# A filter in steps of four rows, copies of every third product input by ScalarE, and a new order, in a tuned convolution and FFN kernel

## The chip, the core and the metric

The kernel runs on one core of a Trainium2 chip. The metric is device time in microseconds (us). The kernel before takes 191.32 us (median of 3 runs, 191.17 to 191.43). The engines are named as in the profile: PE is TensorE (matmuls; PEld its weight loads), DVE is VectorE, ACT is ScalarE, POOL is GpSimd, and SP issues most of the transfers (DMA).

## The reference

For 2048 rows of 640 columns in bfloat16, cut to what matters:

```python
xn = layernorm(A_q)
k_shift = sum over t of 0..3 of A_k shifted down by t rows * A_shift_k[:, t]     # short filter, 4 taps
u = k_shift * A_v
y = causal convolution of u with A_ssm_k along the 2048 rows (by FFT in the reference), in bf16
s = xn * (y + u * A_ssm_D)
g = silu(gelu(xn @ B_w1 + B_b1) @ B_w2 + B_b2)                                    # 640 -> 1728 -> 640
return A_q + s * g
```

## The kernel before

Rows are spread so that partition p holds rows 16p to 16p+15; `n2` is the row within a partition. Two kinds of work run side by side: the FFN, in four chunks of four rows per partition, and the long convolution, done as a Fourier transform of two stages by matrices of sines. Every piece of work is a *step*, a name with a number, and the string `PLAN` lists all steps. `tc.manual_schedule()` keeps that order, so each engine executes its own steps in the order of the plan, and waits at the head of its queue for what the step needs. Nothing overtakes on an engine, and SP issues its transfers in the plan's order too; at most eight of them are under way at a time, since each waits for the landing of the eighth before it.

The steps that the prediction speaks of:

- Loads by SP: `X` (a chunk of A_q), `K` (four rows of A_k a partition, K0 with the rows above), `V` (two rows of A_v), `C` (A_ssm_k, five blocks), `B` (second FFN weight).
- FFN: `tt`/`te` transpose the normalized rows; `h` is the first matmul (L498; five matmuls of 512 columns into one bank, a short one at L494) and `he` its gelu; `g` is the second matmul (L531, fourteen of 320 columns), `ge` its silu, `gm` the multiply into xn.
- Short filter: `cv` with number 8i+s is step s of block i (two rows here) on DVE: products of `kh` with the taps (L626), sums (L622), and in s = 7 the product with v (L615). `uc` is the result, `tm` a temporary, each in a *slot* of `area` of two rows. The taps stand spread over all partitions in `w_exp`: a matmul with a column of the identity makes each half (`tap`, L675), two taps in the opening and two in the late steps `em`, which `ee` copies out.
- Kernel side: `kt` transposes A_ssm_k (L571), `kc` copies out to `kT`, `d` (`add_d`, L672) adds the ssm_D term, `kf` is the first transform stage (L582), `ke` copies out, `ks` stores to DRAM, `fl` loads it back in another layout, `ff` is the second stage, `fe` copies out to `K`, and `mk` loads a copy `ks` of it with neighbouring partitions swapped.
- u side: `uf`, `ue`, `us`, `ml` in the same way, then `mu` the second stage. Its result stays in a PSUM bank; `mp` and `mq` (DVE, L704) multiply it with `K` and `ks` into the two halves of `p`; `ma` and `mb` are the first inverse stage, `me` copies out, `ms` stores.
- End: `yl` loads back, `y` is the second inverse stage (L745, L746), `yt` the gate, `yo`/`ga` add A_q, `ys`/`gs` store.

`ff`, `mu`, `ma` and `mb` come in 40 *units* of 512 columns each. One such step is four matmuls of 32x32 (L445), and `TURNS` says for each unit by how many blocks the output is turned against the input, so that units of different turns occupy different parts of the array. PSUM has eight banks; `one(key)` hands the next free one to a step, and the bank returns when its last reader has dropped it. A slot of `area` is handed out likewise by `Slots.take`, and `SPANNED` names the tiles whose two slots of a pair must lie near each other. `evac` (L143 on ScalarE, L144 on DVE) is the helper that copies PSUM out, as the letter behind a step says.

Of the kernel before, what the change touches and what calls it, by code (L numbers as in the profile page):

```python
# [10 lines left out]
F32 = mybir.dt.float32  # L11
# [6 lines left out]
P = 128  # L18
# [18 lines left out]
cv1 he4 he8 C2 cv0 h6 cv9 he5 lb1 he6 h7 cv2 h12 ln6.d h11 cv8 ln5.d ln4.a h9 he10 ln7.a tt8 he12 B1 cv17 he11 he9 cv3  # L37
he7 cv10 cv18 B0 cv11 cv4 cv19 cv20 tt9 s B2 tt6 tt7 te9.a g3 cv21 te6.d cv22 tt5 C1 ge3 C0 ws2 ss te7.d sm g2 g7 cv12
C3 C4 ge2 kt3 V3 kt5 te5.d kt8 V1 d kc5.d kt10 ws0 kt14 K2 ge7 kc3.a te8.d kc10.d kt0 cv5 kf10 kc8.a kc14.a kf24 kt12
ke24.a kt4 kc12.d kf31 V7 kt6 kf11 kf9 ke10.a K3 kc4.d ke31.a kc0.d ke11.a kf44 kf43 V2 ke44.d kt2 kc2.d kc6.a kf17 X3  # L40
ke9.a kf32 ke32.d kf30 kt11 kf42 kt13 kf37 kt7 kc11.d ke30.a ks10 ke17.a kf38 kc13.d V6 ke42.a ke43.a kt9 ke37.d kf16
kf1 kc7.d kt1 gm3.d kf12 ke38.a ke16.a kc9.d kf36 kt15 kf21 ke1.a ke36.a kc1.d kf6 kf29 gm7.d kc15.d kf39 kf25 ke21.a
X2 cv33 V5 kf20 ke6.a kf41 cv32 V0 cv6 cv24 ks12 ke29.a ks14 cv23 cv13 ke25.a cv34 kf15 ke15.a ke41.a cv56 ke20.a ks5
g5 ke12.a kf7 kf13 ge5 cv57 kf14 kf27 kf8 ke39.a ke27.a kf26 kf40 ke8.a cv41 g0 kf28 ke40.a ks13 ke26.a ke14.a cv40
uf13 kf34 ks3 ke7.a kf19 ge0 cv35 ks8 ue13.a kf18 kf35 ke13.a ke18.a ks4 kf45 g4 ke19.a ks6 gm5.d uf17 cv36 ke45.a kf33
ke34.a ke28.a ks9 ke35.a gm0.d kf0 ke33.a cv7 kf23 cv14 V4 cv58 kf47 cv37 ge4 ke23.a ke0.a kf5 kf22 g6 uf4 ks2 ks11
ke5.a cv42 ke47.a ke22.a ks7 ge6 kf4 kf46 uf5 cv15 ls10 ke4.a cv59 uf15 kf3 ke46.a ks15 kf2 cv38 ke3.a ks1 ke2.a cv25
g1 ue4.a uf0 ks0 ue5.a gm6.d fl0 uf3 ue15.a ue17.a ue3.a uf12 cv43 ue12.a uf14 ue14.a uf16 cv39 ue16.a ue0.a cv26 uf1
# [888 lines left out]
```

## Time and profile before

| | |
|---|---|
| median of the runs | 191.32 us |
| profiled execution | 191.78 us, span 189.8 us |
| busy PE, DVE, ACT, POOL | 183.3, 171.1, 159.1, 59.5 us |
| chain that ended last | PE 75%, DMA 16%, ACT 3%, DVE 2% |
| moved by DMA | 57.67 MB, mean 304 GB/s |
| granted PE clock | full in all slices |

The page sums each engine's busy time, cuts the span into 40 slices, and follows the work that ended last back from release to release. Instructions on one engine overlap a little at their ends, so the time from one start to the next is shorter than the mean duration of one. A busy share is a mean over stages; the windows of the prediction give it stage by stage.

### The profile page before, as it was taken

What the parts mean: (1) busy time and instruction counts of PE and PEld (TensorE: products, weight loads), DVE (VectorE), ACT (ScalarE), POOL (GpSimd) and SP (SyncE); (2) the same over time, 40 slices, a digit from 0 to 9 for tenths busy, and PEclk for the clock granted to TensorE, in tenths of its full rate; (3) what the DMA queues carried; (4) which work ended last, traced back from release to release, by engine and by line L of the source; (5) the groups of instructions that cost most, each with busy time, mean ns of one, the idle gap of its engine ahead of it and who ended that gap; (6) DMA issues with size and microseconds to landing.
All of it is one profiled execution on the core that took longest, in us unless ns stands there. A gap on an engine that the chain in (4) does not pass through costs nothing.

```text
span 189.8 us, 4853 instructions
## 1 busy us (share of the span) xinstructions
PE 183.3 (97%) x1811; PEld 110.0 (58%) x1811; DVE 171.1 (90%) x341; ACT 159.1 (84%) x307; POOL 59.5 (31%) x99
## 2 busy tenths in 40 slices
PE   7999999899999999999999999999999999999992
PEld 2486467787765544466665434467563544677671
DVE  6979999999999999899989999999999950689993
ACT  3469999999999999999988999998789599894031
POOL 8539200013546111266043300046159440001050
PEclk9999999999999999999999999999999999999999
DMA  6999999987998999798599899998988859992165
GB/s 186 397 376 311 363 359 405 380 340 231 391 352 329 254 382 378 234 386 337 178 335 318 266 301 337 310 353 287 343 298 284 287 178 290 402 394 114 38 256 195
DMA packets 26399, 57.67 MB, mean 304 GB/s; under 512 B 3016, under 2 KB 14857, under 8 KB 26376
## 3 DMA queue, kind: packets, MB, share of 16 engines
q1 hardware_dynamic: 21872, 39.65, 61.0%
q0 software_dynamic: 4320, 17.70, 25.1%
q8 instruction: 14, 0.23, 0.5%
q14 instruction: 9, 0.07, 0.1%
q10 hardware_dynamic: 184, 0.01, 0.1%
HBM read 33.76 MB, written 18.35 MB: 275 GB/s over the span
## 4 chain that ended last, share of the span: by engine, by line
PE 75%; DMA 16%; ACT 3%; DVE 2%; issue 1%; SPq 1%; DVEq 0%; ACTq 0%
PE banks L531 28%; PE banks L498 21%; DMA w_sb<-in_B_w_dram 11%; PE banks L582 9%; PE banks L445 8%; DMA area<-in_A_ssm_k_dram 5%; PE banks L746 2%; PE banks L745 2%; PE banks L571 2%; ACT area L143 2%; PE banks L482 1%; ACT hT L510 1%; PE banks L494 1%; DVE xn L555 1%; DVE xn L547 0%
## 5 line engine op out<-in xcount | busy, mean ns | idle before, releaser
L143 ACT CAST area<-banks 128x512 bf16<-128x512 f32 (+3 forms) x162 | 78.8, 618 | 5.5 <-PE banks L445 5.5
L531 PE MATMUL banks<-w_sb,hT 128*128 128x320 bf16 (+1 forms) x462 | 66.0, 295 | 0.1
L531 PEld LDWEIGHTS <-hT 128*128 128x128 bf16 x462 | 43.3, 98 | 19.5 <-issue 3.8
L498 PE MATMUL banks<-xnT,w_sb 128*128 128x512 bf16 x230 | 53.5, 379 | 0.0
L704 DVE TENSOR_TENSOR area<-banks,area 128x512 bf16<-128x512 f32 x80 | 48.6, 682 | 0.8 <-PE banks L445 0.4
L498 PEld LDWEIGHTS <-w_sb 128*128 128x128 bf16 x230 | 21.7, 98 | 25.6 <-issue 2.7
L510 ACT ACTIVATE hT<-banks,b_f 128x512 bf16<-128x512 f32 x52 | 33.9, 706 | 1.8 <-PE banks L498 1.0
L539 ACT ACTIVATE sl<-banks 128x320 bf16<-128x320 f32 (+1 forms) x33 | 14.9, 464 | 12.7 <-PE banks L531 10.9
L626 DVE TENSOR_TENSOR area<-area 128x1280 bf16<-128x1280 bf16 x32 | 25.3, 814 | 0.1
L622 DVE TENSOR_TENSOR area<-area 128x1280 bf16<-128x1280 bf16 x24 | 19.3, 816 | 0.0
L730 POOL DMA_DIRECT2D scrC<-area x16 | 11.8, 737 | 23.2 <-DMA area<-area 18.7
L754 DVE TENSOR_TENSOR area<-banks,xn 128x426 bf16<-128x426 f32 (+1 forms) x18 | 10.0, 595 | 9.1 <-PE banks L746 9.1
L597 POOL DMA_DIRECT2D scrK<-area x16 | 8.8, 555 | 28.7 <-DVE area L144 19.1
L445 PE MATMUL banks<-area,mats 32*32 32x512 bf16 x640 | 17.2, 380 | 0.0
L582 PE MATMUL banks<-area,WA 128*128 128x212 bf16 (+1 forms) x64 | 16.5, 299 | 0.0
L547 POOL TENSOR_TENSOR xn<-xn,sl 128x320 bf16<-128x320 bf16 x14 | 11.2, 808 | 15.6 <-ACT sl L539 10.2
L582 PE MATMUL banks<-area,WB 128*128 128x426 bf16 (+1 forms) x64 | 15.8, 299 | 0.0
L608 POOL DMA_DIRECT2D scrU<-area x16 | 8.6, 543 | 20.9 <-ACT area L143 14.5
L445 PEld LDWEIGHTS <-mats 32*32 32x32 bf16 x640 | 6.4, 88 | 10.1 <-issue 8.2
L763 POOL DMA_DIRECT2D out_dram<-area x6 | 3.3, 551 | 26.5 <-DVE area L759 26.5
L144 DVE CAST area<-banks 128x426 bf16<-128x426 f32 (+3 forms) x18 | 10.9, 611 | 0.7 <-ACT area L143 0.5
L452 DVE BATCH_NORM_STATS2 st<-xn 128x6 f32<-128x320 bf16 x24 | 10.4, 477 | 0.0
(108 smaller groups left out, 209.4 us busy)
## 6 DMA issues: line engine op xcount, KB each, us to landing
scrK<-area POOLq DMA_DIRECT2D x16, 320.0 KB, 4.0
scrU<-area POOLq DMA_DIRECT2D x16, 320.0 KB, 5.1
area<-scrK SPq DMA_DIRECT2D x16, 320.0 KB, 6.6
area<-area SPq DMA_DIRECT2D x32, 160.0 KB, 4.4
area<-scrU SPq DMA_DIRECT2D x16, 320.0 KB, 4.4
scrC<-area POOLq DMA_DIRECT2D x16, 320.0 KB, 4.6
area<-scrC SPq DMA_DIRECT2D x16, 320.0 KB, 6.9
area<-in_A_k_dram SPq DMA_DIRECT2D x4, 640.0 KB, 9.4
```

What stands on the lines that cost most here:

```text
L143: return nc.scalar.copy(out=out_ap, in_=in_ap)
L445: nc.tensor.matmul(out=out[b, :], lhsT=mats[a, m, a], rhs=rhs[a, :], start=start, stop=stop)
L498: nc.tensor.matmul(out=ps, lhsT=w1_sb[:, t, ft * P:(ft + 1) * P], rhs=xnT[:, t, :], start=(t == 0), stop=(t == DT - 1))
L510: nc.scalar.activation(out=hT[:, ft, :], in_=one(("h", i)), func=ACT.Gelu_apprx_tanh, bias=b1_f[:, ft:ft + 1], scale=1.0)
L531: nc.tensor.matmul(out=ps[:, 0:ws.stop - ws.start], lhsT=hT[0:M, ft, q * P:(q + 1) * P], rhs=w2_sb[0:M, ft, hs.start + ws.start:hs.start + ...
L539: nc.scalar.activation(out=sl[:, ws], in_=one(key)[:, 0:ws.stop - ws.start], func=ACT.Silu)
L547: mul.tensor_tensor(out=xr[:, ws], in0=xr[:, ws], in1=live["sl", i][:, ws], op=ALU.mult)
L582: nc.tensor.matmul(out=ps[:, dst], lhsT=(WA, WB)[r][:, n2, :], rhs=rows[:, n2 % 2, src], start=True, stop=True)
L622: nc.vector.tensor_tensor(out=uc, in0=uc, in1=tmp, op=ALU.add)
L626: nc.vector.tensor_tensor(out=tmp if s else uc, in0=kh[:, r0:r0 + KC, :], in1=w_exp[:, j:j + 1, :].to_broadcast([P, KC, D]), op=ALU.mult)
L704: nc.vector.tensor_tensor(out=p_part(i, x), in0=full(one(("mu", i)), i), in1=span(name, i), op=ALU.mult)
L730: nc.gpsimd.dma_start(out=pair_view(scrC)[g2], in_=pair(("c", g2)))
```

## The change

1. `cv` works on blocks of four rows. `quad` takes two slots and makes one access pattern of them (two pieces of two rows); `v`, `uc` and `tm` become SPANNED. There are 32 steps of 2560 elements for 64 of 1280. Their DVE lines are now L641 (products with the taps), L637 (sums) and L630 (times v).
2. Every third unit of u (2, 5, ... 38) gets a step `mv`: ScalarE copies it from PSUM into the half of `p` that `mq` will fill, the bank is free after that one use, and `mp` and `mq` (now L717) read the copy.
3. All four taps are made in the opening, in two rounds over the same four banks, and ScalarE copies them out at full width. `em` and `ee` are gone. Warm-up matmuls go from 6 + 7 to 6 + 2 + 2.
4. Biases of ScalarE are numbers in the instruction; three constant tiles and their memsets are gone.
5. `blocks` knows a form `f`, one full matmul, for units whose turn is 0; the plan marks 61 steps with it.
6. `PLAN` and `TURNS` are written anew. K1 moves from ahead of the C loads to behind them, evacuations and normalizations change between ScalarE and DVE, and the FFN steps are dealt out among the stages in another way.

The diff, cut to its core:

```diff
-WARM = (6, 7)
+WARM = (6, 2, 2)
...
-TURNS = "302320120133202130013212102100231320131321131323"
+TURNS = "303222211332100321313102031211323202233020231231"
...
-ir he0 X1 he1 he2 em6 he3 em7 w h13 em5 K1 ls5 ws1 ls4 ls7 em4 K0 h8 ee6.d ee4.a ls6 h10 ee7.a ee5.a he13 cv16 lv1 lr1
+he2 w X1 ls5 h12 h13 h10 C1 ws1 he12 he4 ls6 h9 ls7 he0 he5 ls4 s he10 he9 K0 lv1 B0 lr1 cv1 lb1 ln7.d ln4.d ln6.d he13
...
-    KV = NJ // KC * 7
+    KV = NJ // KR * 7
...
-    SPANNED = ("kin", "K", "ks", "uin", "c")
+    SPANNED = ("kin", "K", "ks", "uin", "c", "v", "uc", "tm")
...
+    def copied(i):
+        return i % 3 == 2
+
     def one(key):
-        return banks[:, ones.take(key, 2 if key[0] == "mu" else 1), :]
+        return banks[:, ones.take(key, 2 if key[0] == "mu" and not copied(key[1]) else 1), :]
...
-                                 bias=sin_bias[:])
+                                 bias=-math.pi * (1.0 - SIN_EPS))
...
-    def blocks(out, m, rhs, turn, start=True, stop=True):
+    def blocks(out, m, rhs, turn, form, start=True, stop=True):
+        t = int(TURNS[turn])
+        if form == "f" and not t:
+            nc.tensor.matmul(out=out, lhsT=mats[:, m, :], rhs=rhs, start=start, stop=stop)
+            return
...
+    def quad(name, i, uses=1):
+        a0, a1 = (slots.take((name, 2 * i + x), uses) for x in range(2))
+        v = area[:, 2 * a0:2 * a0 + 2, :]
+        return bass.AP(v.tensor, v.offset, [list(v.ap[0]), [2 * D * (a1 - a0), 2], [D, 2], [1, D]])
...
     def kv_step(i):
         i, s = divmod(i, 8)
-        uc = pair(("uc", i), 6)
+        uc = quad("uc", i, 6)
         if s == 7:
-            nc.vector.tensor_tensor(out=uc, in0=uc, in1=pair(("v", i)), op=ALU.mult)
-            slots.drop(("v", i))
+            nc.vector.tensor_tensor(out=uc, in0=uc, in1=quad("v", i), op=ALU.mult)
+            drop_quad("v", i)
             return
...
-            r0 = 3 + i * KC - j
-            nc.vector.tensor_tensor(out=tmp if s else uc, in0=kh[:, r0:r0 + KC, :],
-                                    in1=w_exp[:, j:j + 1, :].to_broadcast([P, KC, D]), op=ALU.mult)
+            r0 = 3 + i * KR - j
+            nc.vector.tensor_tensor(out=tmp if s else uc, in0=kh[:, r0:r0 + KR, :].rearrange("p (a b) d -> p a b d", a=2),
+                                    in1=w_exp[:, j:j + 1, None, :].to_broadcast([P, 2, 2, D]), op=ALU.mult)
...
-    def late_tap(i):
-        tap(i // 2, i % 2, one(("em", i)))
...
+    def u_copy(i):
+        nc.scalar.copy(out=p_part(i, 1), in_=full(one(("mu", i)), i))
+        ones.drop(("mu", i))
+
     def product(i, x):
         name = ("K", "ks")[x]
-        nc.vector.tensor_tensor(out=p_part(i, x), in0=full(one(("mu", i)), i), in1=span(name, i), op=ALU.mult)
+        u = p_part(i, 1) if copied(i) else full(one(("mu", i)), i)
+        nc.vector.tensor_tensor(out=p_part(i, x), in0=u, in1=span(name, i), op=ALU.mult)
         drop_span(name, i)
-        ones.drop(("mu", i))
+        if not copied(i):
+            ones.drop(("mu", i))
...
+        taps(0, 2)
+        warm(WARM[2])
...
+        tap_out(0)
+        tap_out(1)
         norm_dve(0)
         norm_dve(1)
         turn(0)
         turn(1)
-        for j in range(2):
-            for h in range(2):
-                tap(j, h, banks[:, 2 * j + 2 + h, :])
+        taps(2, 4)
```

Three places of the new order, each by the instructions of one engine. First SP in the opening, before: `xn` is A_q, `in_A_k` the K loads, `in_A_ssm_k` the C loads, `w_sb` from `in_B_w` the second FFN weight, `in_A_v` the V loads.

```order
L273 DMA xn<-in_A_q_dram 128x2560
L280 DMA area<-in_A_k_dram 128x2560
L278 DMA area<-in_A_k_dram 112x1920
L279 DMA area<-in_A_k_dram 15x1920
L280 DMA area<-in_A_k_dram 128x2560
L303 DMA area<-in_A_ssm_k_dram 128x2048
L307 DMA w_sb<-in_B_w_dram 128x5x640 x2
L307 DMA w_sb<-in_B_w_dram 128x3x640
L309 DMA w_sb<-in_B_w_dram 64x640
L310 DMA w_sb<-in_B_b_dram 1x640
L303 DMA area<-in_A_ssm_k_dram 128x2048 x4
L283 DMA area<-in_A_v_dram 128x1280 x2
```

The same place now, to the first load of V and the one behind it:

```order
L305 DMA area<-in_A_ssm_k_dram 128x2048
L280 DMA area<-in_A_k_dram 112x1920
L281 DMA area<-in_A_k_dram 15x1920
L282 DMA area<-in_A_k_dram 128x2560
L309 DMA w_sb<-in_B_w_dram 128x5x640 x2
L309 DMA w_sb<-in_B_w_dram 128x3x640
L311 DMA w_sb<-in_B_w_dram 64x640
L312 DMA w_sb<-in_B_b_dram 1x640
L305 DMA area<-in_A_ssm_k_dram 128x2048 x4
L282 DMA area<-in_A_k_dram 128x2560
L275 DMA xn<-in_A_q_dram 128x2560
L282 DMA area<-in_A_k_dram 128x2560
```

One K load stood ahead of the four C loads and stands behind them now: K3, a chunk of A_q and K1 follow, and after them a V load and K2. Second DVE around `add_d`, before; L622 and L626 are filter steps, `mats` the small matrices, the copies to `area` are `kc`.

```order
L626 TENSOR_TENSOR area<-area 128x1280
L144 COPY xnT<-banks 128x512
L622 TENSOR_TENSOR area<-area 128x1280
L144 COPY xnT<-banks 128x512
L425 TENSOR_TENSOR mats<-area 128x384
L622 TENSOR_TENSOR area<-area 128x1280
L144 COPY xnT<-banks 128x512
L672 TENSOR_TENSOR area<-area,dD_sb 128x5
L144 COPY area<-banks 128x640
```

The same place now:

```order
L641 TENSOR_TENSOR area<-area 128x2560
L146 COPY xnT<-banks 128x512 x3
L553 TENSOR_TENSOR xn<-xn,sl_463 128x320
L146 COPY area<-banks 128x640 x3
L553 TENSOR_TENSOR xn<-xn,sl_467 128x320
L146 COPY area<-banks 128x640 x3
L687 TENSOR_TENSOR area<-area,dD_sb 128x5
L553 TENSOR_TENSOR xn<-xn,sl_506 128x320
```

A filter step stood ahead of `add_d` (L672) with a copy between; now six copies of the transposed kernel and two multiplies stand between the last filter step and `add_d` (L687). Third DVE where the products begin, before:

```order
L704 TENSOR_TENSOR area<-banks,area 128x512
L475 TENSOR_SCALAR xn<-xn,mv_1156,rs_1435 128x640
L704 TENSOR_TENSOR area<-banks,area 128x512 x12
L475 TENSOR_SCALAR xn<-xn,mv_1156,rs_1435 128x640
L704 TENSOR_TENSOR area<-banks,area 128x512 x66
```

And now, some way into the same stage:

```order
L717 TENSOR_TENSOR area<-banks,area 128x512 x3
L481 TENSOR_SCALAR xn<-xn,mv_1178,rs_1421 128x640
L717 TENSOR_TENSOR area<-area 128x512
L717 TENSOR_TENSOR area<-banks,area 128x512
L481 TENSOR_SCALAR xn<-xn,mv_1178,rs_1421 128x640
L717 TENSOR_TENSOR area<-banks,area 128x512
L717 TENSOR_TENSOR area<-area 128x512
L717 TENSOR_TENSOR area<-banks,area 128x512 x7
```

Products that read a bank (`banks,area`) are mixed with products whose inputs lie both in `area`; two normalizations stood among 79 products, and four stand there now.

More of the change, by code (lines that the diff above doesn't have):

```diff
@@ L358, in f1_sines @@
             nc.scalar.activation(out=WB[:], in_=prod, func=ACT.Sin, scale=(2.0 * math.pi / L) * (1.0 - SIN_EPS),
-                                 bias=sin_bias[:])
+                                 bias=-math.pi * (1.0 - SIN_EPS))
         elif i == 1:
-            nc.scalar.activation(out=qabs, in_=prod, func=ACT.Abs, scale=1.0, bias=half_l[:])
+            nc.scalar.activation(out=qabs, in_=prod, func=ACT.Abs, scale=1.0, bias=-float(L // 2))
         else:
-            nc.scalar.activation(out=WA[:], in_=qabs, func=ACT.Sin, scale=2.0 * math.pi / L, bias=sin_bias_h[:])
+            nc.scalar.activation(out=WA[:], in_=qabs, func=ACT.Sin, scale=2.0 * math.pi / L, bias=-0.5 * math.pi)
         block_done("s")
@@ L631, in kin_load, with k_f2 @@
         nc.sync.dma_start(out=pair(("kin", g2), 3), in_=pair_view(scrK)[g2])
-    def k_f2(i):
-        blocks(full(one(("ff", i)), i), F2, span("kin", i), i)
+    def k_f2(i, form):
+        blocks(full(one(("ff", i)), i), F2, span("kin", i), i, form)
         drop_span("kin", i)
@@ L659, in i2_sine @@
         nc.scalar.activation(out=GB[:, 4 * i:4 * i + 4, :], in_=i2_index(i, I32), func=ACT.Sin,
-                             scale=(2.0 * math.pi / L) * (1.0 - SIN_EPS), bias=sin_bias[:])
+                             scale=(2.0 * math.pi / L) * (1.0 - SIN_EPS), bias=-math.pi * (1.0 - SIN_EPS))
     def i2_abs(i):
-        nc.scalar.activation(out=i2_index(i, F32), in_=i2_index(i, I32), func=ACT.Abs, scale=1.0, bias=half_l[:])
+        nc.scalar.activation(out=i2_index(i, F32), in_=i2_index(i, I32), func=ACT.Abs, scale=1.0, bias=-float(L // 2))
     def i2_cosine(i):
@@ L693, in swap_load, with u_f2 @@
         slots.drop(("K", g2))
-    def u_f2(i):
-        blocks(full(one(("mu", i)), i), F2, span("uin", i), i)
+    def u_f2(i, form):
+        blocks(full(one(("mu", i)), i), F2, span("uin", i), i, form)
         drop_span("uin", i)
@@ L712, in product_b, with inv1, inv1_a, inv1_b @@
         product(i, 1)
-    def inv1(i, x):
-        blocks(full(one(("mc", i)), i), (I1A, I1B)[x], p_part(i, x), i, x == 0, x == 1)
+    def inv1(i, x, form):
+        blocks(full(one(("mc", i)), i), (I1A, I1B)[x], p_part(i, x), i, form, x == 0, x == 1)
         if x:
             slots.drop(("p", i))
-    def inv1_a(i):
-        inv1(i, 0)
-    def inv1_b(i):
-        inv1(i, 1)
+    def inv1_a(i, form):
+        inv1(i, 0, form)
+    def inv1_b(i, form):
+        inv1(i, 1, form)
     def inv1_out(i, eng):
@@ L779, in sq @@
         def sq(a):
-            nc.scalar.activation(out=sd[:, a:a + 2], in_=mv[:, a:a + 2, 1], func=ACT.Sqrt, bias=eps[:])
+            nc.scalar.activation(out=sd[:, a:a + 2], in_=mv[:, a:a + 2, 1], func=ACT.Sqrt, bias=LN_EPS)
         def rc(a):
@@ L789, in tap_out, with taps @@
         def tap_out(j):
-            nc.scalar.copy(out=halves(w_exp[:, j, :]), in_=banks[:, 2 * j + 2:2 * j + 4, 0:HALF])
+            b = 2 + 2 * (j % 2)
+            nc.scalar.copy(out=halves(w_exp[:, j, :]), in_=banks[:, b:b + 2, 0:HALF])
+        def taps(lo, hi):
+            for j in range(lo, hi):
+                for h in range(2):
+                    tap(j, h, banks[:, 2 + 2 * (j % 2) + h, :])
         def warm(n, bank=7):
@@ L893 @@
         "h": ffn1, "he": ffn1_out, "g": ffn2, "ge": ffn2_silu, "gm": ffn2_mul, "ga": last_add, "gs": last_store,
-        "w": f1_phase, "ws": f1_sines, "d": add_d, "em": late_tap, "ee": late_tap_out,
+        "w": f1_phase, "ws": f1_sines, "d": add_d,
         "s": small_phase, "ss": small_sine, "sm": small_mats,
```

124 lines of the change are left out of this document (60 added, 64 removed).

## The prediction

> **What bounds the kernel now.** I read the page's shares first, then the chain, then a table by stage. The lines of the page: busy time of each engine, PE in 40 slices, DMA rate in the same slices, and the chain by engine.
>
> ```profile
> PE 183.3 (97%) x1811; PEld 110.0 (58%) x1811; DVE 171.1 (90%) x341; ACT 159.1 (84%) x307; POOL 59.5 (31%) x99
> ...
> PE   7999999899999999999999999999999999999992
> ...
> GB/s 186 397 376 311 363 359 405 380 340 231 391 352 329 254 382 378 234 386 337 178 335 318 266 301 337 310 353 287 343 298 284 287 178 290 402 394 114 38 256 195
> ...
> PE 75%; DMA 16%; ACT 3%; DVE 2%; issue 1%; SPq 1%; DVEq 0%; ACTq 0%
> ```
>
> TensorE is the bound: nine tenths or more in nearly every slice, and 75% of the chain. A gain must come out of TensorE's own work or its waits. The windows cut at the stages: opening, filter and first transform (to the first `ff`), second transform of the filter kernel (to the first `mu`), products (to the last `mb`), the round trip through DRAM, the end.
>
> ```profile
> core 0: us, PE busy (x) PEld busy (x) DVE busy (x) ACT busy (x) POOL busy (x), PEclk, DMA share, GB/s
> 9.20:32.40 23.20, 23.20 (x182) 15.78 (x183) 21.81 (x53) 21.48 (x35) 7.17 (x12) 1.00 1.05 363
> 32.40:73.50 41.10, 40.30 (x310) 26.76 (x308) 41.03 (x75) 41.01 (x90) 11.51 (x21) 1.00 0.93 335
> 73.50:97.90 24.40, 24.27 (x270) 14.76 (x269) 22.77 (x53) 23.86 (x51) 9.04 (x15) 1.00 0.85 298
> 97.90:149.40 51.50, 51.41 (x769) 26.16 (x761) 50.72 (x86) 45.22 (x87) 18.68 (x25) 1.00 0.92 312
> 149.40:162.00 12.60, 12.60 (x82) 6.28 (x71) 4.97 (x8) 11.54 (x19) 3.19 (x4) 1.00 0.75 249
> 162.00:185.70 23.70, 23.70 (x189) 17.30 (x187) 21.37 (x45) 12.30 (x22) 3.27 (x6) 1.00 0.63 240
> ```
>
> From 9.2 us on TensorE is idle for hardly 1 us in all. DVE and ScalarE are nearly as full up to 97.9, and DVE again in the product stage (50.72 of 51.50); only after 149.4 do they have air. So work taken from DVE shortens nothing by itself. It lets the order be packed anew, and pays where TensorE waited. Two such places stand in the chain and the timeline.
>
> ```profile
> 1.64 7.51 DMA w_sb<-in_B_w_dram
> ...
> 10.45 13.12 DMA w_sb<-in_B_w_dram
> 23.59 9.29 DMA area<-in_A_ssm_k_dram
> ```
>
> ```profile
> 16.63 0.44 PE L675 MATMUL banks<-skT,ident 4*128 4x320 bf16 x2
> 17.00 0.74 PE L494 MATMUL banks<-xnT,w_sb 128*64 128x256 bf16 x10
> 17.66 0.44 PE L675 MATMUL banks<-skT,ident 4*128 4x320 bf16 x2
> 18.04 0.61 PE L498 MATMUL banks<-xnT,w_sb 128*128 128x512 bf16 x2
> ...
> 32.92 1.40 PEld L571 LDWEIGHTS <-area 128*128 128x128 bf16 x21 [0.21 <-DMA area<-in_A_ssm_k_dram]
> ...
> 35.16 0.53 PE L571 MATMUL banks<-ident,area 128*128 128x128 bf16 x5 [0.71 <-DVE area L672]
> ```
>
> The four late taps sit in the full stretch. The transposes `kt` wait 0.21 for the last load C4 and 0.71 for `add_d` (L672), which stood behind a filter step on DVE.
>
> **The change, part by part.** Unit prices of TensorE come from the chain, those of the other engines from the groups by form, and start to start from merged rows of the timeline.
>
> ```profile
> 40.44 0.31 PE banks L571 x5
> ...
> 46.71 1.90 PE banks L531 x14
> ...
> 59.49 1.08 PE banks L498 x5
> ...
> 64.35 0.18 PE banks L582
> ...
> 65.97 0.67 PE banks L494 x10
> ```
>
> ```profile
> L704 DVE TENSOR_TENSOR area<-banks,area 128x512 bf16<-128x512 f32 x80 | 48.6, 682 | 0.8 <-PE banks L445 0.4 <-ACT area L143 0.2
> L143 ACT CAST area<-banks 128x512 bf16<-128x512 f32 x74 | 40.2, 619 | 5.5 <-PE banks L445 5.5
> ...
> L626 DVE TENSOR_TENSOR area<-area 128x1280 bf16<-128x1280 bf16 x32 | 25.3, 814 | 0.1
> ...
> L445 PE MATMUL banks<-area,mats 32*32 32x512 bf16 x640 | 17.2, 380 | 0.0
> L539 ACT ACTIVATE sl<-banks 128x320 bf16<-128x320 f32 x31 | 14.3, 475 | 11.9 <-PE banks L531 10.1 <-issue 1.7
> ...
> L547 POOL TENSOR_TENSOR xn<-xn,sl 128x320 bf16<-128x320 bf16 x14 | 11.2, 808 | 15.6 <-ACT sl L539 10.2 <-DMA area<-area 5.3
> L452 DVE BATCH_NORM_STATS2 st<-xn 128x6 f32<-128x320 bf16 x24 | 10.4, 477 | 0.0
> ...
> L547 DVE TENSOR_TENSOR xn<-xn,sl 128x320 bf16<-128x320 bf16 x17 | 5.2, 316 | 0.2 <-ACT sl L539 0.2
> ...
> L144 DVE CAST area<-banks 128x512 bf16<-128x512 f32 x6 | 4.0, 676 | 0.0
> ...
> L144 DVE COPY xnT<-banks 128x512 bf16<-128x512 bf16 x9 | 3.5, 419 | 0.7 <-ACT area L143 0.7
> ...
> L475 DVE TENSOR_SCALAR xn<-xn,mv,rs 128x640 bf16<-128x640 bf16 x8 | 3.3, 433 | 0.0
> ```
>
> ```profile
> 24.59 1.55 DVE L626 TENSOR_TENSOR area<-area 128x1280 bf16<-128x1280 bf16 x2
> ...
> 81.41 2.08 ACT L143 CAST area<-banks 128x512 bf16<-128x512 f32 x4
> ...
> 183.01 0.55 DVE L547 TENSOR_TENSOR xn<-xn,sl 128x320 bf16<-128x320 bf16 x2
> ```
>
> *Filter.* A second step of 1280 elements follows the first after 1.55 - 0.81 = 0.74 us, one of 320 after 0.55 - 0.32 = 0.23. The slope is 0.51 / 960 = 0.53 ns an element, so one of 2560 takes 0.74 + 0.67 = 1.41. Thirty-two of these replace 64: 45.1 instead of 47.4, 2.3 us off DVE. TensorE has no part in it. Bounds: two old steps, 1.48, if nothing is saved, and about 3 us if the two pieces of the pattern cost the fast rate (product slope, 0.6 / 512). The row of the same arithmetic is the nearest, so 1.41.
>
> *Copies of u.* Thirteen units (2, 5, ... 38) cost ScalarE (2.08 - 0.62) / 3 = 0.49 each, 6.3 us. Their 26 products now read SBUF alone: 0.23 + 192 x 0.53 ns = 0.33 instead of 48.6 / 80 = 0.61, which takes 7.2 us from DVE. Bounds: 0.23 (the 320 row) and 0.61 (no gain). The copy is one hop more, PE to ACT to DVE; in the order two to twelve DVE instructions stand between a copy and its first product (one only for unit 2), so I cost the hop at nothing; if that cover fails, up to 0.6 us a unit.
>
> *Taps.* The 640-wide copies of taps 2 and 3 go where ScalarE idles before 9.2, ahead of the weight load that lands at 9.15 (1.64 + 7.51). What TensorE gets back is the time from one step's start to the next one's, 16.63 to 17.00 and 17.66 to 18.04, so 0.75, and a little of the gaps ahead of them. Gain 0.8.
>
> *Biases in instructions.* Three memsets of the first microsecond go, which nothing waits for. Nothing.
>
> *Block form.* Each of the 61 steps marked `f` falls on a unit whose turn is not 0, so all 160 units stay four matmuls. Nothing. Three warm-up matmuls go too, in time that waits for the load.
>
> *Order of loads.* K1 (640 KB) leaves the queue ahead of C4. At 363 GB/s that is 1.8 us, so the load's 0.21 goes. In the new order no filter step stands right ahead of `add_d`, and its 0.71 goes. Gain 0.9. What is late next: the loads K1 and K2, below.
>
> *Product stage.* By the plan this stage holds two `g`, three whole `h` and two `ff` fewer, and one short `h` more: 51.41 - 3.8 - 3.2 - 0.2 + 0.7 = 44.9 for TensorE (the work stands elsewhere, where TensorE is full anyway). DVE takes over an evacuation of K, two normalizations and a copy of xnT (0.68 + 0.87 + 0.42 = 2.0): 50.72 - 7.2 + 2.0 = 45.5, and up to 46.3 with the 0.8 that it idled before. So DVE ends this stage, and TensorE waits 0.6 to 1.4 us; I take 1.0. ScalarE: 45.2 + 6.3, less seven evacuations of K (3.4) and four silus (1.9): 46.2 at most, just level.
>
> *Sum:* -0.8 - 0.9 + 1.0 = -0.7 us. The profiled execution took 191.78 (span 189.8, 2.0 around it), 0.46 above the median of 191.32; off the median that is 190.6.
>
> **The rivals.** *DVE does not bind the products.* If the copied product takes the 0.23 of the low bound (2.6 us less), TensorE loses nothing there: -1.7, 189.6. For it: the rate is that of every SBUF row. Against: 512 elements are not 320.
>
> *The moved loads end last (slower).* K1 and K2 now follow C4 (31.1 us), behind K3, X3 and V1: 2.9 MB up to K2's end. At the 335 GB/s of that stage they are there at 39.9. The filter's third quarter wants them at about 41: from 31.6 (32.4 less 0.8) sixteen transposes of 0.31 and thirteen `kf` of 0.18 run to 38.9, the last copy of kT takes 0.4, and one filter step that needs no new load stands between. From there to the last filter step DVE has 26 x 1.41 + four evacuations (2.7) + four multiplies (0.9) + two statistics (1.8) = 42.1; TensorE, up to the first `uf` that needs that step, 70 x 0.18 + 13 x 1.08 + 0.67 + 8 x 1.90 + 0.2 = 42.7. Half a microsecond is all the slack. At the 231 GB/s of one slice K2 comes at 43.9, 2.9 late, of which TensorE feels 2.4: 193.0. It decides from 1.2 us late. The same place punishes a dear filter step: at 1.48 each, 1.8 more less 0.6, 191.8. For it: slices of 178 and 234 exist; against: the slices near 40 us ran at 340 to 231 with the same kind of load.
>
> *The opening doesn't pay.* TensorE comes to the transposes 0.8 earlier, and the load or the sines end there instead: 0.8 of the 1.7 comes, the products take 1.0, and the time is 191.5.
>
> *POOL holds DVE.* The new plan leaves seven POOL multiplies of 0.81 in the product stage. If each held a product that reads two SBUF tensors for its length, 5.7 us would fall on the 26 x 0.33 = 8.6 us of such products in 46, a fifth: 1.1 us, 191.7. The filter steps, which also read two SBUF tensors, average 814 ns over 32 and show no such hold. The Trainium skill (Advanced Engine Details and Errata, section GPSIMD Details) says that the Pool engine shares a read and a write interface with DVE and conflicts with DVE instructions that have two SBUF inputs. By that rule this change makes conflicts that the PSUM products did not have; the trace so far bears it out weakly, so it gets a small chance.
>
> **How the numbers follow.** Forecast 42% (189.9 to 191.1); DVE not binding 16% (188.9 to 189.9); opening doesn't pay 13% (191.0 to 191.8); loads or filter steps late 23% (191.7 to 193.5); POOL 4%; a filter step at the slow rate 2% (far above). About 0.2%, 0.4 us, is what a measurement can tell from no change. Faster: nine tenths of the forecast and all of the second, 55%. Same: the third, and the edges, 18%. Slower: 27%. The range runs from the second case to the middle of the late one, 188.9 to 192.9.
>
> **What would show it.** Transposes that begin near 31.7 without a wait for L687 (the new `add_d`); filter steps near 1.41 start to start; copied products near 0.33; a product stage of 46 us in which DVE is full and TensorE not quite. It is wrong if the chain shows a K load or a filter step ahead of `uf`, if the copied products stay at 0.6, or if TensorE is full in the products.

## The result, and the profile after

| | before | changed |
|---|---|---|
| median of the runs | 191.40 us (191.17 to 191.96) | 193.50 us (190.10 to 193.75) |
| profiled execution, span | 191.78, 189.8 | 193.57, 191.8 |
| ratio changed / before | | 0.9934 (95%: 0.9914 to 0.9954) |

The changed kernel has two times, and the ratio is of the executions near 190.2 alone. The forecast was 190.6. Over both sets of runs there are nineteen executions of the changed kernel: seven at 190.1 to 190.4, two between (191.0 and 192.1), ten at 193.1 to 193.75. The kernel before shows no such split in these runs. So the short executions are some 1.2 us faster than before, and ten of nineteen lose 3.3 us to something else; the first experiment looks for it.

Of the 1.2 us, some 0.2 do not lie in the span, which runs from the first instruction to the last. The time of the kernel before is 2.0 us above its span in all its executions, that of the changed kernel 1.8. Of the kernels below, all but the kernel before with five warm-ups fewer have 1.8 as well, the one that only adds the copies to the kernel before (experiment 3) and the one that only moves its taps (experiment 8) among them. So no part of the prediction explains these 0.2, and where they come from stays open.

The profiled execution is one of the long ones. From its page, busy times, PE in 40 slices, and the chain by engine:

```profile
PE 185.4 (97%) x1797; PEld 111.2 (58%) x1808; DVE 166.1 (87%) x316; ACT 158.7 (83%) x309; POOL 63.3 (33%) x98
...
PE   6999999999999999999999999999999999999992
...
PE 77%; DVE 10%; ACT 6%; issue 2%; DMA 2%; POOL 1%; ACTq 0%
```

DVE has 5.0 us less than before, yet TensorE has 2.1 more with slightly fewer instructions: its matmuls themselves took longer somewhere. The slices do not show where. A short execution (190.24, span 188.5) of the same kernel was profiled in the next set of runs; all further lines of the changed kernel are from it unless the text says otherwise. Its groups:

```profile
L717 DVE TENSOR_TENSOR area<-banks,area 128x512 bf16<-128x512 f32 x54 | 34.4, 678 | 0.1
L641 DVE TENSOR_TENSOR area<-area 128x2560 bf16<-128x2560 bf16 x16 | 23.5, 1482 | 0.0
L637 DVE TENSOR_TENSOR area<-area 128x2560 bf16<-128x2560 bf16 x12 | 17.9, 1491 | 0.2
L451 PE MATMUL banks<-area,mats 32*32 32x512 bf16 x640 | 18.7, 381 | 0.4
L717 DVE TENSOR_TENSOR area<-area 128x512 bf16<-128x512 bf16 x26 | 10.3, 410 | 0.0
L711 ACT CAST area<-banks 128x512 bf16<-128x512 f32 x13 | 7.7, 618 | 0.6 <-PE banks L451 0.6
```

L641 and L637 are the filter's products and sums, L717 the products with u (from a bank, and from a copy), L711 the copies, L451 the blocks of 32x32. There are still 640 of these, so the form `f` was indeed never used. The windows, with the product stage from 99 to 147:

```profile
core 0: us, PE busy (x) PEld busy (x) DVE busy (x) ACT busy (x) POOL busy (x), PEclk, DMA share, GB/s
9.20:32.00 22.80, 22.75 (x189) 15.96 (x188) 20.94 (x48) 19.96 (x30) 6.80 (x7) 1.00 1.04 376
32.00:77.00 45.00, 44.66 (x329) 29.00 (x330) 44.36 (x54) 43.92 (x97) 17.46 (x28) 1.00 0.90 326
77.00:99.00 22.00, 21.93 (x280) 13.83 (x278) 21.67 (x49) 21.41 (x47) 8.49 (x13) 1.00 0.86 297
99.00:147.00 48.00, 47.26 (x727) 23.34 (x734) 47.94 (x97) 45.81 (x90) 16.07 (x21) 1.00 0.92 311
```

As forecast, DVE is full in the products (47.94 of 48) and TensorE not quite (47.26). The first product starts at 99.69 and the last block ends at 145.87, so the stage itself takes some 46 us, as forecast too.

Where the gain came from can be summed on TensorE. I took each matmul's time from its start to the start of the next one, and added these up by shape, for the two profiled executions (191.78 before, 190.24 after):

| | before | after | difference |
|---|---|---|---|
| first matmul of the FFN starts at | 9.19 | 8.57 | -0.62 |
| late taps | 0.74 | none | -0.74 |
| transposes (150 of 128 columns) | 10.58 | 9.82 | -0.76 |
| first transform stage and second inverse stage (192 of 212 to 428 columns) | 27.26 | 26.40 | -0.86 |
| blocks of 32x32 (640) | 16.11 | 17.90 | +1.79 |
| the rest of the FFN | | | 0.0 |
| last matmul starts at | 185.79 | 184.58 | -1.2 |

The 64 matmuls of the second inverse stage take the same in both (8.7), so the 0.86 belong to the first transform stage. The 80 transposes of A_ssm_k alone go from 6.28 to 5.37. The two executions differ by 1.54 us, more than the medians, since the profiled one of before is 0.38 above its median; the table holds 1.2 of it, and 0.24 lie outside the spans.

### The profile page after: what moved, and what is told of

It is laid out like the page before. It is cut to its first block, busy times and chain, and to the rows that moved or that the text cites. A ratio compares the mean times of both kernels' runs of the same rounds, so it can differ in the third digit from the quotient of the medians.

```text
span 191.8 us, 4799 instructions
## 1 busy us (share of the span) xinstructions
PE 185.4 (97%) x1797; PEld 111.2 (58%) x1808; DVE 166.1 (87%) x316; ACT 158.7 (83%) x309; POOL 63.3 (33%) x98
## 3 DMA queue, kind: packets, MB, share of 16 engines
q0 software_dynamic: 4320, 17.70, 25.3%
## 4 chain that ended last, share of the span: by engine, by line
PE 77%; DVE 10%; ACT 6%; issue 2%; DMA 2%; POOL 1%; ACTq 0%
PE banks L537 26%; PE banks L504 21%; PE banks L588 9%; PE banks L451 7%; ACT area L145 4%; PE banks L832 2%; PE banks L760 2%; PE banks L759 2%; DVE area L641 2%; DVE st L458 2%; DMA skp<-in_A_shift_k_dram 2%; PE banks L577 2%; PE banks L690 1%; POOL rs L467 1%; DVE xnT L146 1%
## 5 line engine op out<-in xcount | busy, mean ns | idle before, releaser
L145 ACT CAST area<-banks 128x512 bf16<-128x512 f32 (+2 forms) x153 | 74.5, 591 | 2.8 <-PE banks L451 1.4
L504 PE MATMUL banks<-xnT,w_sb 128*128 128x512 bf16 x219 | 52.4, 379 | 0.7
L516 ACT ACTIVATE hT<-banks,b_f 128x512 bf16<-128x512 f32 x52 | 32.7, 709 | 2.8 <-PE banks L832 1.7
L717 DVE TENSOR_TENSOR area<-banks,area 128x512 bf16<-128x512 f32 x54 | 34.4, 677 | 0.1
L545 ACT ACTIVATE sl<-banks 128x320 bf16<-128x320 f32 (+1 forms) x33 | 14.6, 450 | 14.8 <-PE banks L537 13.0
L553 POOL TENSOR_TENSOR xn<-xn,sl 128x320 bf16<-128x320 bf16 x13 | 10.6, 827 | 48.9 <-ACT sl L545 26.0
L641 DVE TENSOR_TENSOR area<-area 128x2560 bf16<-128x2560 bf16 x16 | 23.5, 1483 | 0.0
L451 PE MATMUL banks<-area,mats 32*32 32x512 bf16 x640 | 18.7, 381 | 0.4
L637 DVE TENSOR_TENSOR area<-area 128x2560 bf16<-128x2560 bf16 x12 | 17.9, 1491 | 0.2
L588 PE MATMUL banks<-area,WA 128*128 128x428 bf16 (+1 forms) x64 | 15.4, 298 | 0.3 <-DVE area L146 0.3
L588 PE MATMUL banks<-area,WB 128*128 128x426 bf16 (+1 forms) x64 | 15.5, 299 | 0.0
L146 DVE CAST area<-banks 128x512 bf16<-128x512 f32 (+2 forms) x23 | 14.2, 635 | 0.1
L451 PEld LDWEIGHTS <-mats 32*32 32x32 bf16 x640 | 6.5, 88 | 10.6 <-issue 8.7
L717 DVE TENSOR_TENSOR area<-area 128x512 bf16<-128x512 bf16 x26 | 10.3, 410 | 0.0
```

Source lines behind the costliest of these rows:

```text
L145: return nc.scalar.copy(out=out_ap, in_=in_ap)
L146: return nc.vector.tensor_copy(out=out_ap, in_=in_ap)
L451: nc.tensor.matmul(out=out[b, :], lhsT=mats[a, m, a], rhs=rhs[a, :], start=start, stop=stop)
L504: nc.tensor.matmul(out=ps, lhsT=w1_sb[:, t, ft * P:(ft + 1) * P], rhs=xnT[:, t, :], start=(t == 0), stop=(t == DT - 1))
L516: nc.scalar.activation(out=hT[:, ft, :], in_=one(("h", i)), func=ACT.Gelu_apprx_tanh, bias=b1_f[:, ft:ft + 1], scale=1.0)
L545: nc.scalar.activation(out=sl[:, ws], in_=one(key)[:, 0:ws.stop - ws.start], func=ACT.Silu)
```

## The experiments

**1. Why two times: the warm-ups.** Warm-ups are matmuls of the identity whose results nobody reads; `WARM` counts those ahead of the small transposes of the tap rows, those behind them, and, where a third number stands, those behind the first taps. The theory (A): ten warm-ups mixed with taps do not always bring TensorE to its full rate. The rival (B): a late load; the long execution has 28 GB/s in one slice near 40 us. Three kernels were run for it. First the changed kernel again, unchanged, for a trace of a short execution.

> The changed kernel once more, unchanged, for a trace of an execution near 190.2 us beside the one of 193.6. If the half rate of TensorE in the opening makes the two times (theory A), the short execution has the 25 first matmuls of 256 columns in about 2.9 us in place of 4.5, and the two executions differ by about 3 us before 14 us and by less than 0.5 after it. If a late load makes them (theory B: the DMA rate of 28 GB/s near 40 us), the openings are alike and the 3 us lie between 35 and 50 us.

It took 190.09 to 193.73 us in twelve executions, six of them above 193. The timeline of TensorE in the opening, first of the long execution (193.57), then of the short one (190.24): L814 are the warm-ups, L690 the taps, L823 the transposes of the rows, L832 the first FFN matmuls.

```profile
4.82 1.03 PE L814 MATMUL banks<-ident 128*128 128x512 bf16 x2
5.79 1.24 PE L690 MATMUL banks<-skT,ident 4*128 4x320 bf16 x4
6.96 1.03 PE L814 MATMUL banks<-ident 128*128 128x512 bf16 x2
7.79 1.27 PE L823 MATMUL banks<-ident,xn 128*128 128x128 bf16 x10
8.99 1.24 PE L690 MATMUL banks<-skT,ident 4*128 4x320 bf16 x4
10.17 4.56 PE L832 MATMUL banks<-xnT,w_sb 128*128 128x256 bf16 x25
```

```profile
4.88 0.85 PE L814 MATMUL banks<-ident 128*128 128x512 bf16 x2
5.72 0.70 PE L690 MATMUL banks<-skT,ident 4*128 4x320 bf16 x4
...
7.18 0.81 PE L823 MATMUL banks<-ident,xn 128*128 128x128 bf16 x10 [0.23 <-DVE xn L800]
7.93 0.71 PE L690 MATMUL banks<-skT,ident 4*128 4x320 bf16 x4
8.57 2.90 PE L832 MATMUL banks<-xnT,w_sb 128*128 128x256 bf16 x25
```

The same instructions take half the time from about 5.7 us on in the short execution; in the long one matmuls of 256 columns start 213 ns apart until 13.6 us, and 107 ns apart from there. Matched matmul by matmul, the long execution is 3.3 us behind the short one at 17 us and 3.3 at its end: nothing is lost after the opening, and the slow slice near 40 us cost nothing. Theory B falls.

Second, two of the three lost warm-ups restored, so that five stand ahead of the first taps and one behind them:

```diff
-WARM = (6, 2, 2)
+WARM = (6, 5, 1)
```

> The changed kernel with WARM = (6, 5, 1) in place of (6, 2, 2): two warm-up matmuls more, and five of the six between the small transposes and the taps. Theory A: TensorE is at full rate when the turns begin, the 25 first matmuls take 2.9 us, every execution is near 190.1 us (0.993 of before), none near 193.6. Theory B: executions of both lengths as before, 190.2 and 193.6.

Six executions, 190.06 to 191.09, none near 193.6; ratio to before 0.9947 (0.9928 to 0.9966). The loss has become rare, but it is not shown to be gone: with the same warm-ups, experiment 4 has one execution of twelve at 193.8, at a mean granted clock of 0.987, and beside it three of 29 executions of the kernel before took 192.9 to 193.3. None of these was profiled. Third, the reverse on the kernel before:

```diff
-WARM = (6, 7)
+WARM = (6, 2)
```

> The kernel before with WARM = (6, 2) in place of (6, 7): five warm-up matmuls fewer, nothing else. Theory A: TensorE stays at half rate until about 10 to 13 us, the 25 first matmuls take up to 4.5 us in place of 2.90, and the time is 2 to 3.5 us longer, about 194 (1.015), in most executions. Theory B: within 0.4 us of before.

Five executions, 194.11 to 195.33, ratio 1.0158 (1.0133 to 1.0183). Its windows:

```profile
4.60:8.00 3.40, 1.36 (x13) 0.63 (x12) 3.04 (x11) 0.98 (x2) 2.76 (x4) 1.00 1.06 397
8.00:14.80 6.80, 6.80 (x34) 4.29 (x32) 3.71 (x16) 3.65 (x6) 2.38 (x5) 0.50 1.06 376
```

Here the granted clock itself says it: 1.00, then 0.50 from 8.0 to 14.8 after a stretch in which TensorE worked 1.36 us of 3.4. The 25 first matmuls took 5.51 us. Warm-ups that seemed to fill a wait for a load were what kept the clock up. The full rate came at 4.6 us in this trace, went 3.4 us later and came back after another 6.8, and in the long execution above it came at 13.6, about 3.4 us after the first FFN matmuls had begun at 10.17. The Trainium skill (TensorE: Matmul & The Clock Gate, Part 1: The HAM clock gate) says that the clock gate, which sets this rate, looks at windows of some 3.4 us that run freely, whatever the kernel does. The traces agree with its length. That one execution in two is long would follow if the phase of the window differs from run to run; no run sets the phase, so this is argued. Between 4.8 and 10.2 us of the long execution TensorE was never idle, and still the rate stayed at half: taps of 4 rows and transposes seem not to count as work enough. The same page of the Trainium skill (Part 4: PE-mode transpose) says of transposes that they do not count as busy in the same way. No run here separates the transposes from the taps.

All kernels below have WARM = (6, 5, 1) unless said otherwise, and are compared with that one (190.06 to 191.09, median 190.47, called the warmed kernel).

**2. The copies of u, undone.** Where a copy stood, the two products of its unit stand now and read the bank.

```diff
     def copied(i):
-        return i % 3 == 2
+        return False
...
-mv2 ... mp2 ... mq2
+mp2 mq2
```

> WARM = (6, 5, 1), and no copies of u: where the copy of a unit stood, its two products stand now and read the bank, as those of the other units do. DVE gains 26 x 0.28 = 7.2 us of work in a stage of 47 us that it already fills to 46.9. If DVE bounds the products, TensorE waits some 6 to 7 us there and the time is 196 to 197 against warm651 (1.03). If the copies only traded one hop for another and TensorE binds, it is within 1 us of warm651.

203.54 us, ratio 1.0625 (1.0605 to 1.0644): 13 us slower, twice the higher of the two expectations. Matched matmul by matmul, it is 0.25 behind the warmed kernel at 98.5 us and 13.6 at 147: all of it in the products. From the groups (the idle time ahead of a group stands last, with what ended most of it) and the windows:

```profile
L717 DVE TENSOR_TENSOR area<-banks,area 128x512 bf16<-128x512 f32 x80 | 49.0, 679 | 5.4 <-DMA area<-area 2.6
...
L451 PE MATMUL banks<-area,mats 32*32 32x512 bf16 x640 | 24.4, 381 | 7.6 <-DVE area L717 6.9
```

```profile
99.00:147.00 48.00, 41.22 (x556) 18.42 (x560) 42.59 (x75) 33.36 (x60) 9.11 (x12) 1.00 0.75 242
```

The added work of DVE (7.2 us expected) is one part; another is 5.4 us in which DVE was idle ahead of products, half of it for the swapped half of K (`area<-area`) that the earlier place doesn't find landed. So this run shows that the order relies on the copies; it doesn't price them alone.

**3. The copies alone, in the old order.** The kernel before (WARM unchanged) with `mv` behind every third `mu`, nothing else moved:

```diff
-mu2 ...
+mu2 mv2 ...
```

> The kernel before with the 13 copies of u alone, each put right behind its matmuls; order otherwise unchanged. DVE has 7.2 us less in the product stage, ScalarE 6.3 us more (45.2 + 6.3 = 51.5 of 51.5). If work taken from DVE shortens nothing where TensorE is full (51.41 of 51.50): within 0.4 us of before. If the copies make ScalarE the bound: 1 to 3 us slower. If DVE did bind: faster by up to 1 us.

203.38 us, ratio 1.0638 (1.0612 to 1.0664): 12 us slower, far from all three. What ended the waits (waiting engine and line, releaser: us in total, times, longest), and one row of ScalarE's timeline; L707 is the copy, L713 the products, L449 the blocks, L535 the second FFN matmul; then the product stage in the windows of before:

```profile
DVE area L713 <- PE banks L449: 8.6, 9, 2.8
ACT area L707 <- PE banks L449: 8.3, 7, 2.7
DVE area L713 <- ACT area L707: 6.4, 7, 2.6
...
PE banks L535 <- ACT area L707: 1.7, 3, 0.7
```

```profile
104.43 0.58 ACT L707 CAST area<-banks 128x512 bf16<-128x512 f32 x1 [2.45 <-PE banks L449]
```

```profile
97.90:149.40 51.50, 45.11 (x599) 22.49 (x614) 37.58 (x69) 42.44 (x81) 10.11 (x14) 1.00 0.76 255
```

ScalarE was not overloaded (42.44 us of 51.50), it was blocked. A copy at the head of its queue waits up to 2.7 us for matmuls to which TensorE has not yet come, and behind it stand the evacuations that TensorE needs to go on. In this order the thirteen copies cost some 0.9 us each.

**4. Does DVE end the products?** The second product of each copied unit cut to 64 of 512 columns:

```diff
-        nc.vector.tensor_tensor(out=p_part(i, x), in0=u, in1=span(name, i), op=ALU.mult)
+        o, k = p_part(i, x), span(name, i)
+        if copied(i) and x:
+            o, u, k = (ap[:, 0:1, 0:64] if len(ap.shape) == 3 else ap[:, 0:64] for ap in (o, u, k))
+        nc.vector.tensor_tensor(out=o, in0=u, in1=k, op=ALU.mult)
```

> WARM = (6, 5, 1), and the second product of each of the 13 copied units works on 64 of its 512 columns (so the output is not the reference's): 13 x 448 x 0.53 ns = 3.1 us less DVE in the product stage, with the same instructions, waits and order. If DVE bounds the products, the 0.74 us that TensorE was idle between 99 and 147 us go, and perhaps some of the rounds of blocks close up: 189.4 to 189.8 against warm651 (190.1 to 190.5). If TensorE's own rounds set the stage, within 0.3 us of warm651.

189.92 to 193.8, median 190.51. Window 99 to 147 of the warmed kernel, then of this one:

```profile
99.00:147.00 48.00, 47.26 (x728) 23.34 (x719) 47.94 (x97) 45.81 (x90) 16.07 (x21) 1.00 0.92 312
```

```profile
99.00:147.00 48.00, 47.02 (x740) 23.18 (x736) 45.84 (x98) 45.73 (x90) 15.61 (x21) 1.00 0.91 308
```

DVE has 2.1 us less (3.1 were expected), and TensorE is no faster. Matmul by matmul, it gains 0.06 us between 111 and 147, behind one wait of 0.3 for a load near 107. A full DVE is not by itself what TensorE waits for.

**5. Or ScalarE?** The copies cut to 64 columns, and in a second kernel the 28 evacuations of the second transform on ScalarE.

```diff
-        nc.scalar.copy(out=p_part(i, 1), in_=full(one(("mu", i)), i))
+        o, u = p_part(i, 1), full(one(("mu", i)), i)
+        o, u = (ap[:, 0:1, 0:64] if len(ap.shape) == 3 else ap[:, 0:64] for ap in (o, u))
+        nc.scalar.copy(out=o, in_=u)
```

> The changed kernel with WARM = (6, 5, 1), and each copy of u takes 64 of its 512 columns (the rest of the unit is stale, so the output is not the reference's): 13 x 448 x 0.84 ns = 4.9 us less ScalarE in the product stage, order and waits the same. If the copies' time on ScalarE is what TensorE waits for in that stage, 0.5 to 1 us below warm651 (0.992 of before or less). If the hop is covered: within 0.3 us of warm651, and the stage's matmuls stand at the same times as there.

```diff
-        evac(eng, span("K", i, 4), full(one(("ff", i)), i))
+        o, f = span("K", i, 4), full(one(("ff", i)), i)
+        if eng == "a":
+            o, f = (ap[:, 0:1, 0:64] if len(ap.shape) == 3 else ap[:, 0:64] for ap in (o, f))
+        evac(eng, o, f)
```

> The changed kernel with WARM = (6, 5, 1), and the 28 evacuations of the kernel's second transform that stand on ScalarE (fe with the letter a) take 64 of 512 columns (the rest of K is stale, so the output is not the reference's): 28 x 448 x 0.84 ns = 10.5 us less ScalarE, nearly all of it between 84 and 112 us, order and waits the same. The block matmuls (32x32) take 17.9 us from start to start in the new order and 16.1 in the old one; the excess stands in the runs at 95, 99, 103 and 106 us. If TensorE waits there for ScalarE to bring the banks back, the block matmuls fall to about 16 us and the time is 1 to 2 us below warm651 (0.985 to 0.99 of before). If the order of the units itself makes the excess (who follows whom, whatever the evacuations take): within 0.3 us of warm651.

190.10 (ratio 0.9938, 0.9923 to 0.9953) and 190.29 (0.9943, 0.9919 to 0.9967), against 0.9947 of the warmed kernel. Matmul by matmul, the short copies gain 0.17 us behind 98 us, in spite of a wait of 0.14 for a load near 106, and the short evacuations 0.15. The window of 95 to 108, where the long waits of the blocks stand, in the warmed kernel, then with short evacuations, and a row of TensorE's waits in the latter:

```profile
95.00:108.00 13.00, 12.66 (x166) 5.19 (x156) 12.93 (x29) 12.96 (x25) 3.31 (x5) 1.00 0.96 300
```

```profile
95.00:108.00 13.00, 12.32 (x170) 5.50 (x170) 12.93 (x30) 9.37 (x25) 3.29 (x4) 1.00 0.96 311
```

```profile
PE banks L451 <- DVE area L146: 0.6, 2, 0.4
```

ScalarE falls from 12.96 to 9.37 of 13, DVE stays at 12.93, and a block then waits for DVE. In the warmed kernel both are full at once, and relieving one of them seems to change who is waited for more than how long. The 1.79 us of the blocks are many short stops: within the runs of blocks, the steps of 100 to 205 ns that wait for a semaphore are 10 before (1.8 us together) and 20 after (3.2), those without one 13 and 11, and steps above 205 ns are eight in both (2.4 and 2.8 us). So most of the growth stands in steps that wait for a semaphore, and little in those that wait for none, where the units' places in the array would show. A kernel that relieves DVE and ScalarE together was not run, so that both together make the stops is argued, not shown. The rival that the last expectation names, the order of the units whatever the evacuations take, stays open: by its mark (within 0.3 us) all three shortened kernels speak for it.

**6. The filter steps.** Each step of 2560 as two of 1280; the sums are shown, and the products with the taps and with v are split likewise:

```diff
...
-            nc.vector.tensor_tensor(out=uc, in0=uc, in1=tmp, op=ALU.add)
+            for a in range(2):
+                nc.vector.tensor_tensor(out=uc[:, a], in0=uc[:, a], in1=tmp[:, a], op=ALU.add)
...
```

> WARM = (6, 5, 1), and each filter step of 2560 elements is two of 1280 at the same place: 32 x 0.07 = 2.2 us more DVE between 14 and 77 us. If DVE sets the pace of that stretch together with TensorE (44.36 and 44.66 busy of 45), the time is 1 to 2 us longer than warm651. If TensorE covers it, within 0.4 us of warm651.

193.54 us, ratio 1.0116 (1.0072 to 1.016): 3.0 slower than the warmed kernel, more than the 2.2 us of DVE work that were expected. Matched with the warmed kernel, nothing is lost up to 68 us; TensorE falls 0.4 behind near 74, 1.4 more by 86, 0.5 more by 92 and 1.2 in the products. What it waited for:

```profile
PE banks L451 <- DVE area L146: 0.5, 2, 0.3
PE banks L588 <- DVE area L632: 0.4, 2, 0.2
PE banks L588 <- DVE area L146: 0.4, 1, 0.4
```

L632 is the multiply by v, the last filter step of a block, ahead of the first transform of u (L588). DVE is as good as full from 32 to 99 us (44.36 of 45 and 21.67 of 22 in the windows above), and work that does not fit shifts until TensorE runs dry.

**7. The loads.** K1 ahead of K0 and of four C loads again:

```diff
-he10 he9 K0 lv1 B0 ... X3 ... K1
+he10 he9 K1 K0 lv1 B0 ... X3 ...
```

> WARM = (6, 5, 1), and the load K1 (640 KB) goes ahead of K0 and so of four C loads, as in the kernel before. C4 lands up to 1.8 us later. If the loads end the wait ahead of the transposes, TensorE waits 0.9 to 1.8 us more there than in warm651. If DVE's copies and sines end it in this order (they stand last in the chain of the new kernel up to 32.8 us), within 0.4 us of warm651.

Median 191.28 (190.92 to 193.08), ratio 0.9998 (0.9968 to 1.0028): 0.8 to 1.0 above the warmed kernel. The profiled execution is its longest, 193.08, so its waits are upper ends:

```profile
PE banks L577 <- DMA area<-in_A_ssm_k_dram: 1.0, 1, 1.0
PE banks L537 <- DMA w_sb<-in_B_w_dram: 0.9, 2, 0.6
```

Both the transposes and an FFN matmul wait for loads behind K1. In the new order the place of K1 is worth 0.8 to 1.0 us; the prediction gave this load 0.21 of its 0.9.

**8. The taps alone.** The kernel before with all taps in the opening, WARM = (6, 5, 1), and without `em` and `ee`:

```diff
-WARM = (6, 7)
+WARM = (6, 5, 1)
...
+        taps(0, 2)
+        warm(WARM[2])
...
-        for j in range(2):
-            for h in range(2):
-                tap(j, h, banks[:, 2 * j + 2 + h, :])
+        taps(2, 4)
```

> The kernel before with all four taps in the opening and WARM = (6, 5, 1), and without the late steps em and ee; the order otherwise unchanged. TensorE loses 0.75 us of matmuls in the full stretch, ScalarE and DVE four half-wide copies. If the opening pays: 0.7 to 0.8 us below before. If the next load or the sines take it back: within 0.3 us of before.

190.76 us, ratio 0.9949 (0.9929 to 0.9969), twelve executions from 190.48 to 191.18. This part alone gives as much as the whole change with its warm-ups (0.9949 and 0.9947), and in both 0.2 us of it lie outside the span. In its profile `add_d` is the longest wait of TensorE behind the start:

```profile
PE banks L571 <- DVE area L672: 0.8, 1, 0.8
```

**9. That wait, taken away.** In the kernel of experiment 8, the filter step `cv12` moves from ahead of `add_d` to behind the copy `kc10`:

```diff
-g7 cv12 C3 C4 ... d kc5.d ... te8.d kc10.d kt0
+g7 C3 C4 ... d kc5.d ... te8.d kc10.d cv12 kt0
```

> The kernel before with all taps in the opening, WARM = (6, 5, 1), and one filter step (cv12) behind add_d and the copy kc10 instead of ahead of add_d; nothing else moved. With the taps alone TensorE still waited 0.84 us for add_d. If that wait was the filter step's, it goes: 0.7 to 0.8 us below the taps alone, about 190.0 (0.991 of before). If the sines or the copies of ScalarE take its place: within 0.3 us of the taps alone.

191.19 us, ratio 0.9997 (0.9975 to 1.0018): no gain. The wait for L672 is gone, and the matmuls at 37.7 us start at the same time as without the move; the first stage needs copies of ScalarE that are no earlier. Near 51 us stands a new one:

```profile
PE banks L582 <- ACT area L143: 0.5, 2, 0.3
```

A wait that another wait hides is worth nothing by itself.

Of the kernels here that compute the whole result, the warmed one has the lowest median. It cannot be told from the kernel before with its taps moved (experiment 8).

## Why the prediction was right, and where it was not

The forecast of 190.6 lies by the executions near 190.2, and the warmed kernel at 190.47 is what it described. That the sum came so near was partly luck: the loss in the blocks was 1.8 us where 1.0 was taken, and a gain of 0.86 in the first transform stage, which the sum does not have, made it good; the 0.62 of the earlier start and the 0.2 outside the span are not in it either. For the other half of the executions the forecast was wrong by 3 us, and they lie above the range of 188.9 to 192.9. One step did it: "Three warm-up matmuls go too, in time that waits for the load." The wait was there, but the warm-ups were not idle filling. Their price was 3.3 us or nothing, and what decides it, as argued above, is the phase of a window. The trace of before had the hint: its warm-ups follow each other by 0.43 us up to 6.4 us and by half of that from there.

- *Filter.* 1.41 us from start to start were forecast for 2560 elements. In the timeline, a step starts at 29.76 and the copy behind it at 31.16:

```profile
29.76 1.48 DVE L641 TENSOR_TENSOR area<-area 128x2560 bf16<-128x2560 bf16 x1
31.16 1.08 DVE L146 COPY xnT<-banks 128x512 bf16<-128x512 bf16 x3
```

  1.40, as worked out from the slope. What filter steps at the old price would cost was put at 1.2 us; experiment 6 measured 3.0.

- *Copies of u.* 0.33 us a copied product; two of them took 0.74 in all (102.77), that is 0.33 and one whole length of 0.41. The copy was forecast at 0.49 and starts 0.48 before the next instruction. The hop was costed at nothing, and in this order copies cut to 64 of 512 columns gain only 0.17 us (experiment 5); experiment 3 shows what it can cost.

```profile
102.77 0.74 DVE L717 TENSOR_TENSOR area<-area 128x512 bf16<-128x512 bf16 x2
```

- *Taps.* 0.8 forecast, 0.74 on TensorE and 0.9 as a whole (experiment 8, 190.76 against 191.63), of which 0.2 lie outside the span. The first FFN matmul came 0.62 earlier besides; 0.33 of that was the wait for a weight load that was late in the profiled execution of before.

- *Order of loads.* 0.9 forecast, and 0.91 measured on the 80 transposes of A_ssm_k. The split of it was off: K1 alone is worth 0.8 to 1.0 in the new order (experiment 7), where 0.21 was forecast. The transposes now begin at 31.07 (31.7 forecast) without a wait for `add_d`; the stop in their place is shorter and DVE's:

```profile
31.07 1.71 PE L577 MATMUL banks<-ident,area 128*128 128x128 bf16 x25
33.02 0.25 PE L588 MATMUL banks<-area,WA 128*128 128x212 bf16 x1 [0.24 <-DVE area L146]
```

  The 0.71 of `add_d` was not simply there for the taking (experiment 9): in the new order it came with K1's move and a place packed anew, and no run separates the two.

- *Product stage.* 1.0 us of loss was taken, and 1.8 came in the blocks. The reason was off as well: "DVE ends this stage". DVE is full, but 2.1 us less of its work bring back no more than 0.1 (experiment 4). What does make the stops is open (experiment 5).

- *First transform.* This term is missing in the sum. The matmuls of L588 take 0.86 us less from start to start than those of L582 before; in experiment 8, which keeps the old order, they do not (18.55 us before and there, 17.70 in the changed kernel). This made good the 0.8 that the blocks lost beyond the 1.0. Which part of the new order brings it no run shows.

- *Rivals.* DVE not binding (189.6): its condition, a copied product of 0.23, did not come (0.33); that less work of DVE brings next to nothing did, but the blocks lost the time all the same. Opening doesn't pay (191.5): it paid (experiment 8). Moved loads late (193.0): the time near 193 was met, by another cause; in the chain of the short execution there is no K load, and the filter steps in it end at 31.2 us, ahead of the transposes and so of every `uf`. POOL: three of the 26 copied products met a multiply on POOL, one of them for its whole length, and took 410 to 414 ns against a median of 410 for all, so DVE was not held. The multiply paid instead: it took 1.07 us beside two such products, against 0.78 to 0.80 for most of the others. The rule of the Trainium skill (Advanced Engine Details and Errata, GPSIMD Details) names a conflict and not who waits. This one case would fit it, with POOL as the one that waits; the trace shows no cost of it to the stage.

## What to carry to other kernels

Matmuls that only fill a wait at the start held TensorE's rate here: before taking one away, look for the place where the time from start to start halves, and afterwards look at all executions, not at the median. Price a copy over a second engine by its place in that engine's queue, where it can block for longer than it lasts (2.45 us for a copy of 0.58), and a removed wait by what would end the same wait next. Where three engines were full at once, less work on one of them bought almost nothing here; taking 0.75 us from TensorE itself gave as much as the whole change.

## What the hardware showed unexpectedly

In the long execution that was profiled, TensorE stayed at half rate through 12 us in which it was hardly idle (12.15 us busy of 12.3 from 1.3 to 13.6, the matmuls of 256 columns at its end 213 ns apart). Ten executions of nineteen have its time. The profile's row of the granted clock read full there, and 0.50 only where the rate had been full and fell back (8.0 to 14.8 us of the kernel before with five warm-ups fewer). In the traces of the kernels with twelve or thirteen warm-ups the full rate set in anywhere between 4.0 and 6.9 us, so the time from start to start is the view to trust in an opening.
